# Retention attention and a SwiGLU block on one core: another order for the first 160 steps, and a last block in halves

## The chip, the core and the metric

The kernel runs on one core of a Trainium2 chip. The metric is the device time of one execution in microseconds, so less is better. The engines are TensorE (PE, with its weight loads shown apart as PEld), VectorE (DVE), ScalarE (ACT), GpSimd (POOL) and SyncE (SP), which here only issues transfers. Each engine works through its own queue in order and waits on semaphores where it needs another engine's or a transfer's result.

## What is computed

```python
# q, k, v: (4, 8, 768, 64) float32; gamma per head
for t in range(S):
    state = gamma * state + outer(k[:, :, t], v[:, :, t])
    y[:, :, t] = scale * q[:, :, t] @ state
x = y.transpose(0, 2, 1, 3).reshape(4 * 768, 512)
g, val = x @ w_gate, x @ w_val          # w_gate, w_val: (512, 1536)
out = (silu(g) * val) @ w_out           # w_out: (1536, 512)
```

The three weight matrices come as 64-bit floats, and the kernel converts them itself.

## The kernel before

The 3072 tokens are worked on in four segments (0 to 3) of six blocks of 128 tokens: three chunks of 128 positions of two sequences. Each segment has its attention, an "up" stage (x times the gate and value weights, for 12 pieces of 128 columns of d_ff) and a "down" stage (times w_out). Every float32 product with the weights is made as three matmuls, of operands that are split beforehand into three parts `a` = 0, 1, 2: part 0 by ScalarE (`near_a`, `far_a`), part 1 by VectorE (`near_b`, `far_b`), part 2 by GpSimd or VectorE (`near_c`, `far_c`). In segments 1 to 3 the up stage uses seven block products for eight, from weights that segment 0 has prepared and written to DRAM (`wup`, `wdn`, `wdnt`).

The order of all work is written out by hand in one list, `PLAN`. Its entries are called one after another, and each entry issues its instructions to the queues of its engines, so the list fixes the order within every queue. The start, which is segment 0, has these entries (n is a chunk or a piece of weights):

- On SP, transfers: `l n:w` loads chunk n (w = 0 k transposed, 1 q transposed, 2 v, 3 k; 256 KB each), `A0 A1 A2` the table of decays (256 KB each; A0 and A1 are the mask, A2 the factors for q and k), `U n` and `V n` the 64-bit words of a weight piece (512 KB for each of its halves), `Z n` writes a prepared piece to DRAM, `L` two tiny loads of decay factors.
- Attention of chunk n: `s` scores (TensorE, then two mask products on VectorE), `m` scores times v (TensorE, then ScalarE's part 0 of x), `x n:1` and `x n:2` the other two parts of x (VectorE), `k` or `K` scaling of k on GpSimd or VectorE, `q` or `Q` the same of q, `t` the new state (TensorE, then ScalarE or VectorE), `o` the old state's share (TensorE), `g` decay of the state (ScalarE), `h` copies of the table (ScalarE).
- Weights of piece n: `a`, `b`, `S`, `c`, `C` convert 64-bit words to float32 (a, b, c on ScalarE, S and C on VectorE; for pieces 12 and up, which are w_out, C is on GpSimd), `T` differences of blocks for the seven products (VectorE), `n n:0` to `n n:2` the three parts of the gate weights, `n n:3` to `n n:5` those of the value weights (ScalarE, VectorE, GpSimd in turn).
- Products: `p f:j` gate and `v f:j` value, for pieces 0 and 1 and token blocks j, 12 matmuls each; `u`, `y` their silu and product; `G`, `W`, `i`, `j` the same for the later pieces.

In the down stage `s/D f.tok` (`down`) adds piece f to the bank of token block tok with three matmuls, `s/W f` (`w_load`) loads the split w_out rows of piece f (768 KB), `s/h f` (`h_split`) splits the hidden values, and `s/e tok` (`finish`) scales the finished bank on ScalarE or VectorE and stores it. The last entries of the list are `3/D10.2 3/D11.2 3/e2`: token block 2 is the last. Block 5 of the last segment is already scaled by two engines, a half each, and stored by two transfers.

Of the kernel before, what the change touches and what calls it, by code (L numbers as in the profile page):

```python
# [26 lines left out]
TH = L * P
NSEG = B * NCK // (2 * L)
# [19 lines left out]


PLAN = """  # L50
    l1:0 A2 l0:0 A1 A0 l0:2 U0:0 l2:1 l0:3 s0 a0:1 l2:0 s1 m0 K0 b0:1 V0:0 S0:1 c0:1 l1:2 x0:2 s2
    l1:3 l3:0 x0:1 C0:1 l3:1 k1 U1:1 l2:3 t0 l2:2 l4:0 a0:0 g2 n0:0 Q2 l4:1 n0:1 m1 b0:0 S0:0 c0:0
    n0:2 t1 x1:1 a1:1 l3:3 x1:2 o2 C0:0 a1:0 s3 b1:1 S1:1 l3:2 q3 l5:1 n0:3 n0:4 c1:1 p0:0 l5:2 k2
    l5:0 o3 C1:1 m2 n0:5 t2 s4 b1:0 k3 v0:0 x2:2 S1:0 u0:0 g3 l4:2 U2:0 c1:0 m3 n1:0 U12:3 x2:1 t3
    C1:0 s5 q5 n1:1 h0 q4 o5 o4 x3:1 x3:2 m4 T0:0 n1:3 y0:0 T0:1 m5 p0:1 v0:1 a2 x4:1 u0:1 x5:2 U3:1
    n1:4 T1:0 y0:1 n1:2 T1:1 b2 p1:0 T0:2 U4:0 n1:5 u1:0 a12 Z0 p1:1 a3 x4:2 v1:0 x5:1 v1:1 y1:0
    p0:2 u1:1 v0:2 S2 U5:1 b12 c2 p1:2 u0:2 S12 T1:2 y1:1 C2 n2:0 n2:3 v1:2 y0:2 Z1 b3 n2:1 u1:2
    n2:2 S3 n2:4 T2:0 c3 a4 U13:2 G2:1 C3 y1:2 U6:0 T2:1 n3:0 G2:0 b4 n2:5 n3:1 i2:0 i2:1 T2:2 c12
    W2:0 j2:0 n3:2 W2:1 G3:1 n3:3 S4 C12 a5 Z2 j2:1 Z12 n3:4 c4 C4 U7:1 n3:5 T3:0 T3:1 c13 T3:2 G3:0
    n4:0 n4:1 b5 S5 n4:2 W3:0 n4:3 W3:1 i3:0 i3:1 n4:4 a13 a6 G4:1 c5 Z3 b13 G4:0 T4:0 U8:0 C5 T4:1  # L60
    j3:1 n4:5 b6 U14:3 W4:1 n5:0 T4:2 n5:1 i4:1 n5:2 n5:3 j3:0 S6 i4:0 a7 c6 n5:4 W4:0 T5:0 C6 G5:1
    Z4 T5:1 n6:0 L U9:1 j4:0 n5:5 S13 G5:0 a8 b7 n6:3 T5:2 j4:1 n6:1 c14 C13 W5:1 S7 i5:1 Z5 n6:4
    i5:0 n6:2 j5:1 c7 W5:0 G6:1 n6:5 l4:3 a9 U10:0 C7 n7:0 G6:0 j5:0 i6:1 T6:0 k4 b8 g4 Z13 n7:1
    n7:3 U15:2 S8 n7:2 W6:1 i6:0 c8 n7:4 T7:0 a14 W6:0 C8 l5:3 T7:1 T6:1 b14 G7:1 U11:1 n8:0 n8:1
    n7:5 i7:1 T6:2 G7:0 j6:0 b9 S14 W7:0 h2 c15 j6:1 Z6 S9 C14 n8:3 c9 n8:2 i7:0 n8:4 W7:1 G8:1 T7:2
    C9 G8:0 j7:0 n8:5 a10 b10 n9:0 j7:1 n9:3 Z14 a15 W8:0 P2 W8:1 Z7 n9:4 k5 b15 i8:0 S10 T8:0 n9:1
    i8:1 U16:3 n9:5 c10 S15 P0 T8:1 n9:2 C10 a11 C15 G9:0 t4 G9:1 P1 T9:0 i9:0 T8:2 Z15 j8:1 g5 j8:0
    t5 W9:1 W9:0 b11 n10:0 U17:2 T9:1 c16 Z8 n10:3 1/was0.0 a16 i9:1 n10:1 n10:4 n10:2 b16 G10:1 S11
    n10:5 c11 S16 i10:1 G10:0 0/h0.0 j9:0 C16 Z16 C11 n11:0 W10:0 n11:3 a17 j9:1 i10:0 0/h0.1 b17
# [237 lines left out]
T0, UP0 = 30.0, 8.35  # L307
# [61 lines left out]
def tile_retnet_swiglu(  # L369
# [13 lines left out]
    nc = tc.nc  # L383
# [20 lines left out]
    def f32(t):  # L404
        return t.bitcast(F32)
# [28 lines left out]
    banks = [two[:, ts(i - 4, 512)] if i in (4, 5) else  # L434
             psum.tile([P, 512], F32, name=f"bank{i}") for i in range(8)]
# [532 lines left out]
    def far_a(o, x):  # L968
        act(o[0], x, AF.Copy, scale=CUT)
# [112 lines left out]
    hs, wo = {}, {}  # L1082
# [14 lines left out]
    def w_load(s, t, f, first):  # L1097
        def load():
            wo[f] = item("o", DM)
            o = wo[f].bitcast(U32)  # L1100
            if first:
                nc.sync.dma_start(out=o[:, 2], in_=w_dn[f].bitcast(U32))
            else:
                nc.sync.dma_start(out=o, in_=w_dn3[f])
# [12 lines left out]
    def down(f, tok):
        i, u = divmod(tok, L)
        for a in range(3):
            nc.tensor.matmul(banks[tok], hs[f][:, a, ds(i * TH + u * P, P)], wo[f][:, a],  # L1120
                             start=f == a == 0, stop=f == NF - 1 and a == 2,
                             skip_group_check=True)

    def finish(s, tok):
        i, u = divmod(tok, L)
        p, pos = divmod(s * L, NCK)
        row = (2 * p + i) * S + (pos + u) * P
        t = chunk_x[:, ts(tok % 4, DM)]
        if s == NSEG - 1 and tok > 3:
            t = tmp[:, ts(tok - 4, DM)]  # L1130
        scale = ONE * ONE
        if s == NSEG - 1 and tok == 5:
            a, b = (ds(n * DM // 2, DM // 2) for n in range(2))
            act(t[:, a], banks[tok][:, a], AF.Copy, scale=scale)
            nc.scalar.dma_start(out=out[ds(row, P), a], in_=t[:, a])
            nc.vector.tensor_scalar(t[:, b], banks[tok][:, b], scale, None, op0=mul)
            nc.sync.dma_start(out=out[ds(row, P), b], in_=t[:, b])
            return
        if tok % 2:
            nc.vector.tensor_scalar(t, banks[tok], scale, None, op0=mul)  # L1140
        else:
            act(t, banks[tok], AF.Copy, scale=scale)  # L1142
        nc.sync.dma_start(out=out[ds(row, P)], in_=t)
# [11 lines left out]
    def down_stage(s, t):  # L1155
        nxt = s + 1 if s + 1 < NSEG else None
        table = {**WHEN, **FIRST} if s == 0 else WHEN
        slot_at, steps = [], []
        for n in range(6 * NF):
            f, b = divmod(n, 6)  # L1160
            slot_at.append(t)
            if b == 0:
                steps.append(t)
            if nxt and n in PARTS:
                what, p = PARTS[n]
                d = t + COST[what] + 0.1
                if what == "s":
                    at(t, f"{nxt}/sc{p}", scores_of, p, (R0, R0 + 1) if p else (4, 5))
                    for i in range(2):
                        at(d + 0.1 * i, f"{nxt}/dec{p}.{i}", decayed, p, i)  # L1170
                        at(d + 0.2 + 0.1 * i, f"{nxt}/q{p}.{i}", scale_q2, p, i)
                    if has_old(nxt, p, 0):
                        at(d + 0.6, f"{nxt}/was{p}.0", decay2, nxt, p, 0)
                    if p == 0:
                        at(d + 0.7, f"{nxt}/begin", begin_x, nxt)
                else:
                    k = "ABC".index(what)
                    z = k // 2
                    for i in range(0 if k else 2):
                        at(t - 0.02 + 0.01 * i, f"{nxt}/k{p}.{i}", scale_k2, p, i)  # L1180
                    at(t, f"{nxt}/{what}{p}", (mix_a, mix_b, mix_c)[k], nxt, p)
                    if k != 1 and has_new(nxt, p, z):
                        at(d, f"{nxt}/new{p}.{z}", keep_state, nxt, p, z)
                    if k == 1 and has_new(nxt, p, 1):
                        at(d + 0.9, f"{nxt}/was{p}.1", decay2, nxt, p, 1)
                    for j in range(8 if k else 0):
                        at(d + 0.1 * j, f"{nxt}/y{p}.{z}{j}", bring_y, z, j % 2, j // 2 % 2, j // 4)
                    if k == 2:
                        make_x(d + 1.0, nxt, p, table)
                t += COST[what]  # L1190
            tok = b
            at(t, f"{s}/D{f}.{tok}", down, f, tok)
            t += 3 * PASS_D
            if f == NF - 1:
                at(t + WHEN["end" if nxt else "last"][tok], f"{s}/e{tok}", finish, s, tok)
        for f in range(NF):
            h_split(s, steps[f], f, table["h", f if nxt else NF])
            w_load(s, steps[f], f, s == 0)
        if nxt:
            for n, h in LOADS.items():  # L1200
                at(slot_at[h] + 1.0, f"{nxt}/l{n}", load_pair, nxt, n)
            for f in range(3):
                at(slot_at[UNITS[f]], f"{nxt}/L{f}", load_unit, f)
        return t
# [30 lines left out]
    t = down_stage(0, end)  # L1235
    for s in range(1, NSEG):
# [8 lines left out]
        t = down_stage(s, t)  # L1245
# [50 lines left out]
```

## Time and profile before

| | |
|---|---|
| median of 3 runs | 645.15 us (644.22 to 645.72) |
| the profiled execution | 643.87 us |
| its span, first to last instruction | 642.1 us |
| TensorE busy | 632.8 us, 99% of the span |
| VectorE, ScalarE, GpSimd busy | 76%, 61%, 41% |
| transfers | 140.13 MB, mean 218 GB/s |
| granted TensorE clock | 1.000 |

In the profile's rows a time is in microseconds from the start of the span. In the timeline and the chain a row gives the start, the length, the engine, the line of the kernel and the tile that is written and read; "[1.52 <-DMA x]" says that the engine stood idle for 1.52 us before and that a transfer of x ended this. "SPq" is a transfer's issue on SP's queue; the list of issues gives the size and the time from issue to landing.

### The profile page before, as it was taken

What the parts mean: (1) busy time and instruction counts of PE and PEld (TensorE: products, weight loads), DVE (VectorE), ACT (ScalarE), POOL (GpSimd) and SP (SyncE); (2) the same over time, 40 slices, a digit from 0 to 9 for tenths busy, and PEclk for the clock granted to TensorE, in tenths of its full rate; (3) what the DMA queues carried; (4) which work ended last, traced back from release to release, by engine and by line L of the source; (5) the groups of instructions that cost most, each with busy time, mean ns of one, the idle gap of its engine ahead of it and who ended that gap; (6) DMA issues with size and microseconds to landing.
All of it is one profiled execution on the core that took longest, in us unless ns stands there. A gap on an engine that the chain in (4) does not pass through costs nothing.

```text
span 642.1 us, 14098 instructions
## 1 busy us (share of the span) xinstructions
PE 632.8 (99%) x5576; PEld 580.2 (90%) x5576; DVE 487.8 (76%) x712; ACT 391.8 (61%) x860; POOL 264.5 (41%) x174
## 2 busy tenths in 40 slices
PE   7999999999999999999999999999999999999997
PEld 6899999987779999997778999998777999999886
DVE  4988887999898887665787869675789866778361
ACT  3678797777865565666766555564785555654121
POOL 0625555554436875630003665550101666653000
PEclk9999999999999999999999999999999999999999
DMA  9989988789787445258775640457767444304554
GB/s 320 375 290 338 317 320 290 281 290 328 259 283 298 170 151 173 69 171 270 248 240 213 198 164 8 183 196 247 241 223 264 155 163 173 115 0 157 195 184 170
DMA packets 50050, 140.13 MB, mean 218 GB/s; under 512 B 4928, under 2 KB 17472, under 8 KB 49984
## 3 DMA queue, kind: packets, MB, share of 16 engines
q1 hardware_dynamic: 49552, 138.57, 62.7%
q8 instruction: 44, 0.72, 0.5%
q10 hardware_dynamic: 432, 0.66, 0.3%
q14 instruction: 22, 0.18, 0.1%
HBM read 109.32 MB, written 29.88 MB: 217 GB/s over the span
## 4 chain that ended last, share of the span: by engine, by line
PE 97%; DMA 2%; SPq 0%; POOL 0%; ACT 0%; issue 0%; POOLq 0%
PE bank L1057 41%; PE bank L1120 32%; PE bank L888 13%; PE bank L758 6%; PE bank L906 3%; DMA hT<-in_k_n_dram 1%; DMA tab<-in_decays_dram 1%; PE bank L713 1%; PE bank L699 1%; PE bank L628 1%; PE bank L684 0%; POOL hT L649 0%; SPq L586 0%; SPq L464 0%; ACT chunk_x L1142 0%
## 5 line engine op out<-in xcount | busy, mean ns | idle before, releaser
L1120 PE MATMUL bank<-oitem,gitem 128*128 128x512 f32 x864 | 208.5, 395 | 0.0
L1120 PEld LDWEIGHTS bank<-oitem,gitem 128*128 128x128 f32 x864 | 159.0, 188 | 35.3 <-DMA oitem<-wdnt 0.5
L966 POOL TENSOR_TENSOR gitem<-gitem 128x768 fp32r<-128x768 f32 x72 | 140.6, 1963 | 116.6 <-DVE gitem L963 98.6
L1057 PE MATMUL bank<-xa,gitem 128*128 128x384 f32 x864 | 160.5, 334 | 0.0
L1057 PEld LDWEIGHTS bank<-xa,gitem 128*128 128x128 f32 x864 | 150.8, 188 | 0.2
L966 POOL TENSOR_TENSOR oitem<-oitem 128x256 fp32r<-128x256 f32 (+1 forms) x60 | 65.7, 1102 | 53.0 <-DVE oitem L963 51.2
L1057 PE MATMUL bank<-xb,gitem 128*128 128x384 f32 x432 | 84.5, 334 | 0.0
L888 PE MATMUL bank<-xa,oitem 128*128 128x384 f32 x480 | 84.4, 335 | 0.0
L888 PEld LDWEIGHTS bank<-xa,oitem 128*128 128x128 f32 x480 | 83.0, 188 | 0.4 <-DVE hT L442 0.2
L963 DVE SCALAR_TENSOR_TENSOR gitem<-gitem,loads 128x768 fp32r<-128x768 f32 x72 | 75.1, 1058 | 9.2 <-ACT gitem L960 7.8
L1057 PEld LDWEIGHTS bank<-xb,gitem 128*128 128x128 f32 x432 | 75.9, 188 | 0.4
L960 ACT ACTIVATE gitem<-loads 128x768 fp32r<-128x768 f32 x72 | 59.6, 843 | 25.9 <-PE bank L1057 16.8
L963 DVE SCALAR_TENSOR_TENSOR gitem<-gitem,hT 128x768 fp32r<-128x768 f32 x48 | 46.2, 965 | 25.4 <-ACT gitem L960 25.4
L960 ACT ACTIVATE gitem<-hT 128x768 fp32r<-128x768 f32 x48 | 40.2, 841 | 32.4 <-PE bank L1120 30.2
L991 ACT COPY chunk_x<-bank 64x128 f32<-64x128 f32 x144 | 36.6, 260 | 31.9 <-PE bank L758 21.1
L399 DVE SCALAR_TENSOR_TENSOR gitem<-gitem 128x768 fp32r<-128x768 f32 x48 | 49.1, 1030 | 0.8
L785 POOL TENSOR_TENSOR loads<-loads,tab 128x512 f32<-128x512 f32 x9 | 13.3, 1475 | 81.7 <-PE bank L758 44.6
L1057 PE MATMUL bank<-xb,oitem 128*128 128x384 f32 x216 | 43.4, 335 | 0.0
L1057 PEld LDWEIGHTS bank<-xb,oitem 128*128 128x128 f32 x216 | 38.0, 188 | 0.3
L1074 DVE TENSOR_TENSOR hT<-bank,tmp 128x384 f32<-128x384 f32 x36 | 20.0, 554 | 20.1 <-PE bank L1057 19.9
L963 DVE SCALAR_TENSOR_TENSOR oitem<-oitem,loads 128x256 fp32r<-128x256 f32 (+1 forms) x42 | 34.1, 816 | 0.9 <-ACT oitem L960 0.8
L1072 ACT COPY tmp<-bank 128x384 f32<-128x384 f32 x36 | 17.2, 478 | 27.9 <-PE bank L1057 18.9
(112 smaller groups left out, 792.3 us busy)
## 6 DMA issues: line engine op xcount, KB each, us to landing
loads<-wup SPq DMA_DIRECT2D x36, 896.0 KB, 4.7
oitem<-wdnt SPq DMA_DIRECT2D x36, 768.0 KB, 4.4
wdnt<-oitem SPq DMA_DIRECT2D x12, 768.0 KB, 5.9
wup<-first SPq DMA_DIRECT2D x9, 896.0 KB, 5.5
rawp<-in_w_gate_dram SPq DMA_DIRECT2D x12, 512.0 KB, 6.6
rawp<-in_w_val_dram SPq DMA_DIRECT2D x12, 512.0 KB, 6.2
rawp<-in_w_out_dram SPq DMA_DIRECT2D x12, 512.0 KB, 6.8
out_dram<-chunk_x SPq DMA_DIRECT2D x22, 256.0 KB, 2.2
```

Of the source, the lines that this page charges most:

```text
L399: stt(o, x, 1.0, y, op0=mul, op1=op)
L758: nc.tensor.matmul(o, a, b, start=start, stop=True, skip_group_check=True)
L888: nc.tensor.matmul(o, w[:, a, ts(b, P)], X0[:, a, i, NC - 1 - b], start=a == b == 0, stop=a == 2 and b == NC - 1, skip_group_check=True)
L906: nc.tensor.matmul(o, w[:, a, ts(b, P)], X0[:, a, :, NC - 1 - b, ts(j, P)], start=a == b == 0, stop=a == 2 and b == NC - 1, skip_group_che ...
L960: act(o[0], x, AF.Copy, scale=CUT / FAR)
L963: stt(o[1], f32(o[0]), -FAR, x, op0=mul, op1=add)
L966: op(o[2], f32(o[0]), f32(o[1]), op=add)
L991: copy(cx[half[i], ds(2 * h, 2), c, half[z]], y.rearrange("p (b t) -> p b t", b=2))
L1057: nc.tensor.matmul(o, w[:, a, k], x[:, a, KH - 1 - k], start=start and a == k == 0, stop=a == 2 and k == KH - 1, skip_group_check=True)
L1072: steps = (lambda: copy(p1, x), lambda: tt(c11, z, p1, op=add), lambda: act(gate, c11, AF.Silu, scale=ONE), lambda: copy(u2, x), lambda: c ...
L1074: lambda: copy(p5, wb), lambda: tt(h1, x, p5, op=add),
L1120: nc.tensor.matmul(banks[tok], hs[f][:, a, ds(i * TH + u * P, P)], wo[f][:, a], start=f == a == 0, stop=f == NF - 1 and a == 2, skip_group ...
```

## The change

Three things are changed. The first 160 entries of `PLAN` are put in the order of the kernel that this one was made from; the entries after them keep their order (`L` and `l5:3`, which stood further back, come into the first 160). The last token block of the last segment (`FINAL`, block 2) gets its last three products as six matmuls of half the columns, and its scaling and store as two halves, one on VectorE and SP, one on ScalarE and its queue. Of the w_out loads of the last segment the first three go as two transfers, of two thirds and of one third. `down` gets the segment as an argument for this.

```diff
@@ -48,22 +48,22 @@
 
 
 PLAN = """
-    l1:0 A2 l0:0 A1 A0 l0:2 U0:0 l2:1 l0:3 s0 a0:1 l2:0 s1 m0 K0 b0:1 V0:0 S0:1 c0:1 l1:2 x0:2 s2
-    l1:3 l3:0 x0:1 C0:1 l3:1 k1 U1:1 l2:3 t0 l2:2 l4:0 a0:0 g2 n0:0 Q2 l4:1 n0:1 m1 b0:0 S0:0 c0:0
-    n0:2 t1 x1:1 a1:1 l3:3 x1:2 o2 C0:0 a1:0 s3 b1:1 S1:1 l3:2 q3 l5:1 n0:3 n0:4 c1:1 p0:0 l5:2 k2
-    l5:0 o3 C1:1 m2 n0:5 t2 s4 b1:0 k3 v0:0 x2:2 S1:0 u0:0 g3 l4:2 U2:0 c1:0 m3 n1:0 U12:3 x2:1 t3
-    C1:0 s5 q5 n1:1 h0 q4 o5 o4 x3:1 x3:2 m4 T0:0 n1:3 y0:0 T0:1 m5 p0:1 v0:1 a2 x4:1 u0:1 x5:2 U3:1
-    n1:4 T1:0 y0:1 n1:2 T1:1 b2 p1:0 T0:2 U4:0 n1:5 u1:0 a12 Z0 p1:1 a3 x4:2 v1:0 x5:1 v1:1 y1:0
-    p0:2 u1:1 v0:2 S2 U5:1 b12 c2 p1:2 u0:2 S12 T1:2 y1:1 C2 n2:0 n2:3 v1:2 y0:2 Z1 b3 n2:1 u1:2
-    n2:2 S3 n2:4 T2:0 c3 a4 U13:2 G2:1 C3 y1:2 U6:0 T2:1 n3:0 G2:0 b4 n2:5 n3:1 i2:0 i2:1 T2:2 c12
-    W2:0 j2:0 n3:2 W2:1 G3:1 n3:3 S4 C12 a5 Z2 j2:1 Z12 n3:4 c4 C4 U7:1 n3:5 T3:0 T3:1 c13 T3:2 G3:0
-    n4:0 n4:1 b5 S5 n4:2 W3:0 n4:3 W3:1 i3:0 i3:1 n4:4 a13 a6 G4:1 c5 Z3 b13 G4:0 T4:0 U8:0 C5 T4:1
-    j3:1 n4:5 b6 U14:3 W4:1 n5:0 T4:2 n5:1 i4:1 n5:2 n5:3 j3:0 S6 i4:0 a7 c6 n5:4 W4:0 T5:0 C6 G5:1
-    Z4 T5:1 n6:0 L U9:1 j4:0 n5:5 S13 G5:0 a8 b7 n6:3 T5:2 j4:1 n6:1 c14 C13 W5:1 S7 i5:1 Z5 n6:4
+    l0:0 l1:0 A0 A1 s0 U0:0 l0:2 l0:3 a0:1 s1 b0:1 A2 h0 S0:1 m0 K0 x0:2 c0:1 l2:0 x0:1 l2:1 l1:3
+    C0:1 t0 l1:2 V0:0 l3:1 n0:0 s2 a0:0 Q2 l3:0 l2:3 n0:1 b0:0 S0:0 m1 k1 x1:1 x1:2 l2:2 c0:0 n0:2
+    U1:1 C0:0 t1 o2 l3:3 g2 s3 n0:3 n0:4 l4:1 p0:0 m2 a1:1 x2:1 k2 q3 b1:1 l4:0 a1:0 x2:2 S1:1 l5:1
+    l3:2 n0:5 c1:1 k3 t2 C1:1 o3 b1:0 l5:0 l4:2 g3 v0:0 s4 S1:0 t3 l5:2 c1:0 C1:0 U2:0 m3 s5 U12:3
+    U3:1 q5 q4 u0:0 a2 o5 o4 T0:0 n1:0 m4 b2 y0:0 x3:1 x3:2 m5 T0:1 n1:1 n1:3 T0:2 S2 n1:2 p0:1 v0:1
+    n1:4 T1:0 x4:1 u0:1 y0:1 a12 n1:5 x5:1 U4:0 T1:1 a3 p1:0 x4:2 u1:0 p1:1 x5:2 Z0 u1:1 T1:2 c12
+    v1:0 U5:1 y1:0 v1:1 p0:2 Z1 l5:3 v0:2 c2 C2 b12 y1:1 p1:2 n2:0 a4 U6:0 u0:2 b3 n2:1 u1:2 v1:2
+    S12 n2:3 L y0:2 S3 c3 n2:2 U13:2 G2:0 n2:4 T2:0 G2:1 C3 y1:2 T2:1 n3:0 b4 n2:5 n3:1 i2:0 i2:1
+    T2:2 W2:0 j2:0 n3:2 W2:1 G3:1 n3:3 S4 C12 a5 Z2 j2:1 Z12 n3:4 c4 C4 U7:1 n3:5 T3:0 T3:1 c13 T3:2
+    G3:0 n4:0 n4:1 b5 S5 n4:2 W3:0 n4:3 W3:1 i3:0 i3:1 n4:4 a13 a6 G4:1 c5 Z3 b13 G4:0 T4:0 U8:0 C5
+    T4:1 j3:1 n4:5 b6 U14:3 W4:1 n5:0 T4:2 n5:1 i4:1 n5:2 n5:3 j3:0 S6 i4:0 a7 c6 n5:4 W4:0 T5:0 C6
+    G5:1 Z4 T5:1 n6:0 U9:1 j4:0 n5:5 S13 G5:0 a8 b7 n6:3 T5:2 j4:1 n6:1 c14 C13 W5:1 S7 i5:1 Z5 n6:4
     i5:0 n6:2 j5:1 c7 W5:0 G6:1 n6:5 l4:3 a9 U10:0 C7 n7:0 G6:0 j5:0 i6:1 T6:0 k4 b8 g4 Z13 n7:1
-    n7:3 U15:2 S8 n7:2 W6:1 i6:0 c8 n7:4 T7:0 a14 W6:0 C8 l5:3 T7:1 T6:1 b14 G7:1 U11:1 n8:0 n8:1
-    n7:5 i7:1 T6:2 G7:0 j6:0 b9 S14 W7:0 h2 c15 j6:1 Z6 S9 C14 n8:3 c9 n8:2 i7:0 n8:4 W7:1 G8:1 T7:2
-    C9 G8:0 j7:0 n8:5 a10 b10 n9:0 j7:1 n9:3 Z14 a15 W8:0 P2 W8:1 Z7 n9:4 k5 b15 i8:0 S10 T8:0 n9:1
+    n7:3 U15:2 S8 n7:2 W6:1 i6:0 c8 n7:4 T7:0 a14 W6:0 C8 T7:1 T6:1 b14 G7:1 U11:1 n8:0 n8:1 n7:5
+    i7:1 T6:2 G7:0 j6:0 b9 S14 W7:0 h2 c15 j6:1 Z6 S9 C14 n8:3 c9 n8:2 i7:0 n8:4 W7:1 G8:1 T7:2 C9
+    G8:0 j7:0 n8:5 a10 b10 n9:0 j7:1 n9:3 Z14 a15 W8:0 P2 W8:1 Z7 n9:4 k5 b15 i8:0 S10 T8:0 n9:1
     i8:1 U16:3 n9:5 c10 S15 P0 T8:1 n9:2 C10 a11 C15 G9:0 t4 G9:1 P1 T9:0 i9:0 T8:2 Z15 j8:1 g5 j8:0
     t5 W9:1 W9:0 b11 n10:0 U17:2 T9:1 c16 Z8 n10:3 1/was0.0 a16 i9:1 n10:1 n10:4 n10:2 b16 G10:1 S11
     n10:5 c11 S16 i10:1 G10:0 0/h0.0 j9:0 C16 Z16 C11 n11:0 W10:0 n11:3 a17 j9:1 i10:0 0/h0.1 b17
@@ -1101,7 +1101,8 @@
             if first:
                 nc.sync.dma_start(out=o[:, 2], in_=w_dn[f].bitcast(U32))
             else:
-                nc.sync.dma_start(out=o, in_=w_dn3[f])
+                for i in (slice(2), slice(2, 3)) if s == NSEG - 1 and f < 3 else (slice(None),):
+                    nc.sync.dma_start(out=o[:, i], in_=w_dn3[f][:, i])
 
         def o():
             return [wo[f][:, i] for i in range(3)]
@@ -1114,12 +1115,17 @@
             at(t + c, f"{s}/d{f}.2", lambda: far_c(o(), f32(o()[2])))
             at(t + z, f"{s}/Z{f}", lambda: nc.sync.dma_start(out=w_dn3[f], in_=wo[f].bitcast(U32)))
 
-    def down(f, tok):
+    halves_of = [ds(n * DM // 2, DM // 2) for n in range(2)]
+    FINAL = 2
+
+    def down(s, f, tok):
         i, u = divmod(tok, L)
-        for a in range(3):
-            nc.tensor.matmul(banks[tok], hs[f][:, a, ds(i * TH + u * P, P)], wo[f][:, a],
-                             start=f == a == 0, stop=f == NF - 1 and a == 2,
-                             skip_group_check=True)
+        final = s == NSEG - 1 and f == NF - 1 and tok == FINAL
+        for cols in halves_of if final else [slice(None)]:
+            for a in range(3):
+                nc.tensor.matmul(banks[tok][:, cols], hs[f][:, a, ds(i * TH + u * P, P)],
+                                 wo[f][:, a, cols], start=f == a == 0,
+                                 stop=f == NF - 1 and a == 2, skip_group_check=True)
 
     def finish(s, tok):
         i, u = divmod(tok, L)
@@ -1130,11 +1136,18 @@
             t = tmp[:, ts(tok - 4, DM)]
         scale = ONE * ONE
         if s == NSEG - 1 and tok == 5:
-            a, b = (ds(n * DM // 2, DM // 2) for n in range(2))
+            a, b = halves_of
             act(t[:, a], banks[tok][:, a], AF.Copy, scale=scale)
             nc.scalar.dma_start(out=out[ds(row, P), a], in_=t[:, a])
             nc.vector.tensor_scalar(t[:, b], banks[tok][:, b], scale, None, op0=mul)
             nc.sync.dma_start(out=out[ds(row, P), b], in_=t[:, b])
+            return
+        if s == NSEG - 1 and tok == FINAL:
+            a, b = halves_of
+            nc.vector.tensor_scalar(t[:, a], banks[tok][:, a], scale, None, op0=mul)
+            nc.sync.dma_start(out=out[ds(row, P), a], in_=t[:, a])
+            act(t[:, b], banks[tok][:, b], AF.Copy, scale=scale)
+            nc.scalar.dma_start(out=out[ds(row, P), b], in_=t[:, b])
             return
         if tok % 2:
             nc.vector.tensor_scalar(t, banks[tok], scale, None, op0=mul)
@@ -1189,7 +1202,7 @@
                         make_x(d + 1.0, nxt, p, table)
                 t += COST[what]
             tok = b
-            at(t, f"{s}/D{f}.{tok}", down, f, tok)
+            at(t, f"{s}/D{f}.{tok}", down, s, f, tok)
             t += 3 * PASS_D
             if f == NF - 1:
                 at(t + WHEN["end" if nxt else "last"][tok], f"{s}/e{tok}", finish, s, tok)
```

## The prediction

> **What bounds the kernel now.** I read the page first, then the chain of work that ended last, then the first 35 us and the last 10 us of the timeline.
>
> ```profile
> span 642.1 us, 14098 instructions
> PE 632.8 (99%) x5576; PEld 580.2 (90%) x5576; DVE 487.8 (76%) x712; ACT 391.8 (61%) x860; POOL 264.5 (41%) x174
> PE 97%; DMA 2%; SPq 0%; POOL 0%; ACT 0%; issue 0%; POOLq 0%
> ```
>
> TensorE (PE) is busy all but 9.3 us of the span (642.1 less 632.8). A change that leaves the amount of matmul alone can only work on those 9.3 us, or add to them. The chain in order of time says where they lie:
>
> ```profile
> 8.06 7.49 DMA hT<-in_k_n_dram
> ...
> 15.69 1.05 POOL hT L649
> ...
> 16.79 0.69 PE bank L684 x16
> 17.48 1.02 PE bank L699 x16
> 18.50 1.09 PE bank L628 x16
> 19.59 1.62 PE bank L906 x12
> ...
> 22.23 1.02 PE bank L713 x16
> 23.25 0.47 PE bank L684 x16
> ...
> 29.01 1.89 PE bank L699 x32
> 30.90 1.90 PE bank L713 x32
> 32.80 14.59 PE bank L906 x120
> ...
> 590.66 47.66 PE bank L1120 x210
> 638.34 0.60 ACT chunk_x L1142
> ```
>
> From 16.79 until ScalarE's copy at 638.34 the chain is TensorE alone, one step after another without a hole that counts. Ahead of it stands one load (a k_n chunk, issued at 8.06, landed at 15.55), then GpSimd's scaling of it (step k1), then the matmuls that use it (t1). So two places count: what makes TensorE unbroken at the start, and what follows its last matmul.
>
> In these rows s (scores) is L628, t (state) L684, o (old state) L699, m (mix) L713, p and v (first gate and value products) L906. Their costs on the chain are 1.09, 0.47 (0.69 once), 1.02, 1.02 and 1.62 us.
>
> The start is bound by loading:
>
> ```profile
> 5.00:10.00 5.00, 3.33 (x30) 3.36 (x32) 1.22 (x2) 0.00 (x0) 0.00 (x0) 1.00 1.05 382
> 20.00:25.00 5.00, 5.00 (x77) 4.51 (x76) 4.33 (x9) 3.90 (x7) 2.83 (x4) 1.00 1.05 386
> 12.04 0.69 DVE L649 TENSOR_TENSOR hT<-hT,tab 128x512 f32<-128x512 f32 x1 [0.43 <-DMA hT<-in_k_n_dram]
> 12.84 1.16 PE L628 MATMUL bank<-hT 64*128 64x128 f32 x16 [1.52 <-DMA hT<-in_k_t_dram]
> 14.92 1.09 PE L713 MATMUL bank<-tmp,hT 128*64 128x128 f32 x16 [0.30 <-DMA hT<-in_v_n_dram]
> 22.16 0.85 PEld L713 LDWEIGHTS bank<-tmp,hT 128*64 128x64 f32 x16 [0.17 <-DMA hT<-in_v_n_dram]
> ```
>
> The last two columns of the windows are the DMA share (full) and GB/s. At 386 GB/s a block of 256 KB (a chunk, or a third of the table) takes 262,144 B / 386 GB/s = 0.68 us and a weight half twice that. One queue, SP's, issues nearly all of it, so a load lands when its place in the queue comes up. Counting places in 256 KB in the old order: l2:0 is place 11, l1:2 place 14, l1:3 place 15 and l2:2 place 23; the rows show them at about 12.8, 14.9, 15.55 and 22.1. The bytes do not change, so the same places should land at the same times in the new order, whoever stands in them.
>
> **The change, part by part: the first 160 steps.** TensorE's own order changes little: t0 goes ahead of s2, m2 and t2 ahead of o3, v0:0 ahead of s4. What changes is the places:
> - l1:2 goes from 14 to 13, l1:3 from 15 to 12, l2:2 from 23 to 19, V0 from 13 to 15; a block of the table, A2, from 2 to 9.
> - l3:0 is at 17 (was 16), l4:0 at 26 (was 24), l3:2 at 28 (was 27), l5:0 at 29 (was 30).
>
> t0, now ahead of s2, waits for K0 on VectorE (0.69), and K0 for the late A2: place 9, 15.55 - 6 x 0.68 = 11.5, so K0 ends at 12.2 and t0 at about 12.8, which is when s2 can start anyway. t1, the step that released everything before, now has k_n at 12: 15.55 - 3 x 0.68 = 13.5, plus 1.05 of GpSimd = 14.6. m1 has its v at 14.2 and runs to 15.3, so t1 runs right behind it, 15.3 to 15.9, and not at 16.79. o2 needs Q2 on VectorE, behind the two mask products of s2:
>
> ```profile
> 14.93 0.70 ACT L532 ACTIVATE first<-rawp 128x512 f32<-128x512 f32 x1
> 16.44 0.84 DVE L643 TENSOR_TENSOR loads<-hT,tab 128x512 f32<-128x512 f32 x1
> 17.57 0.59 ACT L535 ACTIVATE bank<-first 128x512 int32<-128x512 f32 x1
> 18.20 0.70 DVE L545 SCALAR_TENSOR_TENSOR bank<-first,bank 128x512 uint32<-128x512 uint32 x1 [0.28 <-ACT bank L535]
> 18.93 0.69 ACT L538 ACTIVATE first<-rawp 128x512 int32<-128x512 uint32 x1 [0.76 <-DVE bank L545]
> 20.00 0.68 DVE L553 CUSTOM_DVE_ANT_0 first<-bank,first 128x1024 uint16<-128x1024 uint16 x1
> 20.60 1.27 DVE L634 TENSOR_TENSOR tmp<-bank,tab 128x512 f32<-128x512 f32 x2
> 22.27 0.61 ACT L960 ACTIVATE oitem<-first 128x512 fp32r<-128x512 f32 x1
> 23.74 1.27 POOL L966 TENSOR_TENSOR oitem<-oitem 128x512 fp32r<-128x512 f32 x1 [1.36 <-DVE oitem L963]
> ```
>
> s2 keeps its data at places 10 and 11 and so its 12.84; its products end at 14.0, the masks 1.27 later, Q2 0.84 later: 16.1. o2 runs 16.1 to 17.1. What is late next is l3:0: place 17, 15.55 + 2 x 0.68 = 16.9. So s3 starts at 17.1 (18.50 before). Behind it: s3 1.09, p0:0 1.62, m2 1.02, t2 0.47, o3 1.02, v0:0 1.62, to 23.9. l4:0 at place 26 lands at 22.1 + 3 x 0.68 = 24.1: s4 to 25.2, t3 to 25.7. l3:2 at place 28 is there at 25.5, m3 ends at 26.7; s5 has l5:0 at 26.2 and ends at 27.8; o5 and o4 1.89 and m4 and m5 1.90 more: 31.6. Then p0:1 starts, the first of the 120 matmuls that began at 32.80. **Gain 1.2 us, and I take 1.1**, since several steps (s4, s5) come to rest within 0.3 us of what releases them.
>
> The conversions must keep up. For the value weights (V0, place 15, 15.55) the steps above are a, b, S, c, C, n:3 and n:5, in this order by time except that a is the first row; n:4 is another 0.68 on VectorE. In the new order: a to 16.25, b 16.85, S 17.55, c 18.25; C waits behind two splits of x (0.68 each) to 19.5; n0:3 20.1; behind the mask products of s3, n0:4 at 21.4; n0:5 at 22.7. v0:0 starts at 22.3 and needs that last part after two thirds, at 23.4. That is 0.7 us of cover; when it is gone TensorE waits.
>
> After 31.6 everything is to arrive 1.1 us earlier than before. The tightest place I found in the old order is G2:1:
>
> ```profile
> 46.39 1.30 POOL L966 TENSOR_TENSOR oitem<-oitem 128x512 fp32r<-128x512 f32 x1 [9.20 <-DVE oitem L963]
> 47.11 12.97 PEld L888 LDWEIGHTS bank<-xa,oitem 128*128 128x128 f32 x75
> ```
>
> GpSimd ends at 47.69, and the product wants that part eight matmuls after 47.1, about 48.5: 0.8 us spare, less than the gain. But the new order puts a2, b2 and S2 well ahead of the splits of x (S2 was step 132, now 106), so the conversion for G2 ends earlier too. On ScalarE a2 now waits for U2, place 35, 22.1 + 12 x 0.68 = 30.3, with n1:0, m4's copy, b2 and m5's copy queued behind it; a2 is twice the 0.70 row, so n1:0 starts at about 31.7, and p1:0, which wants it, comes at 31.6 + 2 x 1.46 = 34.5: hidden. The moves of L (two tiny loads), l5:3 (256 KB, no wait in front of it), h0 (a copy on ScalarE ahead of m0's copy, while that waits for its matmuls) and c12 I cost at nothing: ScalarE is busy 61% of the span. Without that cover c12 would cost two of the 0.69 row, 1.4 us, and l5:3 one place, 0.7.
>
> **The last block in halves.** Rows of the old end, where another block (tok 5) is in halves already:
>
> ```profile
> 636.11 0.38 ACT L1134 ACTIVATE tmp<-bank 128x256 f32<-128x256 f32 x1
> 636.52 0.42 DVE L1136 TENSOR_SCALAR tmp<-bank 128x256 f32<-128x256 f32 x1 [2.93 <-ACT tmp L1134]
> ...
> out_dram<-chunk_x SPq DMA_DIRECT2D x1, 256.0 KB, 2.0
> ...
> out_dram<-tmp ACTq DMA_DIRECT2D x1, 128.0 KB, 2.1
> ```
>
> VectorE had been idle for 2.93 us, and the block's products were done, since ScalarE was at its half already; yet VectorE's half began only when that ended: the two halves of one bank went one behind the other. In the change the order is VectorE first, ScalarE second. So behind the last matmul come 0.42 + 0.03 + 0.38 = 0.83 us in place of 0.60: +0.23. The six half-width matmuls cost 6 x 14.59/120 = 0.73 against 3 x 47.66/210 = 0.68: +0.05. The store is half as long but lands no sooner, 2.1 against 2.0: +0.1. **Tail +0.35.** Bounds: with all halves free of each other, VectorE's would lie beside the second half's matmuls, and only ScalarE's 0.38 stays: +0.05 - 0.22 + 0.1 = -0.07.
>
> The rows show two readers of a bank in series; none shows a reader of one half while TensorE writes the other. Here the Trainium skill (PSUM — Partial Sum Buffer, section "PSUM bank collisions raise a hardware error") speaks against the change: two engines on one bank and quadrant collide even at disjoint columns, TensorE's writes included, so accesses are kept apart in time. By that rule VectorE's half would wait for all six matmuls, and the tail is the +0.35; by halves alone it would be the -0.07. No run yet shows the mixed pair.
>
> **Three w_out loads in two.**
>
> ```profile
> oitem<-wdnt SPq DMA_DIRECT2D x36, 768.0 KB, 4.4
> 590.50 6.78 PE L1120 MATMUL bank<-oitem,gitem 128*128 128x512 f32 x29
> 590.74 0.32 SPq L1104 DMA_DIRECT2D oitem<-wdnt  x1
> ```
>
> W2 is issued at 590.74 and lands at 595.1; its first product is the tenth block of three matmuls after 590.50, at 590.50 + 27 x 0.227 = 596.6. One more issue of 0.32 us fits in 1.5 us. SP has only stores of finished blocks and later loads behind it. Cost 0; without that cover, 0.3 each.
>
> **Sum.** Profiled execution: 643.87 us, of which 642.1 is the span. -1.1 + 0.35 = -0.75, so 643.1 there. The three runs have the median 645.15, 1.28 above the profiled one; against it the forecast is 645.15 - 0.75 = **644.4 us**.
>
> **The rivals.**
> - *The halves overlap* (-0.07, not +0.35): 645.15 - 1.1 - 0.1 = 643.95. For it: the products of the two halves are separate groups. Against: the 2.93 us row. Chance 0.2.
> - *The gain is used up on the way*: some conversion between 35 and 130 us, not TensorE, turns out to set the pace, and only some 0.2 us of the lead are left; with the tail 645.3. For it: 0.8 us spare at G2:1. Against: no wait there now, VectorE and ScalarE both get the weights of G2 earlier. Chance 0.17.
> - *Slower: the value weights come too late.* V0 lands about 1.4 us later than before. From its a (14.93) to the end of n0:5 (23.74 + 1.27) the old rows take 10.1 us, because work for other pieces stood between. If the new order kept those 10.1, n0:5 would end at 25.7, v0:0 could start at 24.6 instead of 22.3, and p0:1, 9.1 us of steps later, at 33.7, 0.9 later than before; with the tail 645.15 + 1.25 = 646.4, and more if k3, next on GpSimd, holds up t3 as well. It decides once n0:5 ends after 23.4. Against: in the old order g2, a1:1, a1:0 and b1:1 stood on ScalarE inside this chain, in the new one they stand behind n0:3 (g2 alone before it). Chance 0.18.
> - *The places mean nothing*: loads land as before whatever their order, and only the tail acts: 645.5. Against: four rows that fit one line. Chance 0.05.
>
> **How the numbers follow.** Forecast 0.4. Its own doubt is about 0.9 us either way: if only l3:0 binds, p0:1 starts at 31.4 and the start gives 1.4; each block that lands later than its place takes 0.7. A measurement of this kernel tells about 0.2%, 1.3 us, from no change: the bounds are 643.86 and 646.44. Faster: half of the overlap case (0.1) and some 0.4 of the forecast's (0.17): 0.27. Slower: half of the late weights (0.1), and as much again from the tails of the used-up lead and the others: 0.2. Same: 0.53. The range goes from 643.1 (overlap, and a start 0.8 better) to 646.4 (the late weights as priced) and leaves out what lies above.
>
> **What would show it.** s3 at about 17.1 and p0:1 at about 31.6; t1 no longer on the chain; a load (l3:0, l4:0 or l3:2) as the last wait. At the end VectorE's half starting after the last matmul, ScalarE's after VectorE's, and about 4 us from last matmul to end of span. Wrong: p0:1 later than 32.8, n0:5 ending after 23.4, a wait of TensorE between 35 and 130 us, or VectorE's half starting under the last three matmuls.

## The result, and the profile after

The changed kernel takes 643.19 us in the median (642.66 to 644.22), the kernel before 645.2 us in the same comparison (644.22 to 645.72). The ratio is 0.9971, 95% interval 0.9959 to 0.9982: faster by 2.0 us, with 1.2 to 2.6 inside the interval. The forecast was 644.4, in a range of 643.1 to 646.4; the time lies at its lower edge, and the sign went to the case that had been given 0.27.

The profiled execution of the changed kernel took 642.91 us, that of the one before 643.87: 0.96 less. The page after, its first lines:

```profile
span 641.1 us, 14110 instructions
PE 631.2 (98%) x5579; PEld 579.5 (90%) x5579; DVE 485.6 (76%) x713; ACT 392.2 (61%) x860; POOL 265.4 (41%) x174
PE 94%; DMA 4%; ACT 0%; DVE 0%; SPq 0%; issue 0%; ACTq 0%
```

TensorE is still the bound; the holes are 9.9 us (641.1 less 631.2), no smaller than before. What changed is where the chain begins to be TensorE alone. The chain in order of time, after, as the profile puts it together:

```profile
6.96 6.04 DMA hT<-in_k_n_dram
...
13.02 9.00 DMA rawp<-in_w_gate_dram
...
22.04 0.69 ACT first L532
...
22.75 0.61 ACT bank L535
...
23.38 0.71 DVE bank L545
...
24.11 0.68 ACT first L538
...
24.81 0.70 DVE first L553
...
25.65 0.69 PE bank L684 x16
26.33 0.88 PE bank L713 x16
27.21 1.09 PE bank L628 x16
28.30 1.89 PE bank L699 x32
30.19 1.90 PE bank L713 x32
32.09 0.91 PE bank L906 x6
```

Before, a k_n chunk and GpSimd's scaling released TensorE at 16.79. Now TensorE is unbroken from t3 on, at 25.65. p0:1, the last row, starts at 32.09 and not at 32.80: 0.71 us won. The timeline has the same stretch with its waits:

```profile
16.61 1.16 PE L628 MATMUL bank<-hT 64*128 64x128 f32 x16
17.70 1.70 PE L906 MATMUL bank<-xa,oitem 128*128 128x256 f32 x12
20.90 1.27 POOL L966 TENSOR_TENSOR oitem<-oitem 128x512 fp32r<-128x512 f32 x1 [1.15 <-DVE oitem L963]
21.84 1.69 PE L906 MATMUL bank<-xa,oitem 128*128 128x256 f32 x12
24.18 1.16 PE L628 MATMUL bank<-hT 64*128 64x128 f32 x16 [0.65 <-DMA hT<-in_k_t_dram]
25.65 0.69 PE L684 MATMUL bank<-hT 128*64 128x64 f32 x16 [0.30 <-DVE first L553]
```

These are s3, p0:0, the last part n0:5 of the first value weights, v0:0, s4 and t3. Up to s4 it went as forecast, to 0.1 us, or a little better; t3 came 0.45 later than forecast.

What releases t3 has to be read with care. The chain names a weight transfer, the gate half of U1, and its five conversion steps (a1:1, b1:1, S1:1, c1:1, C1:1), because C1:1 is what ended last before t3 began. But t3 does not need C1:1. In the kernel C1:1 reads bank 7 and t3 writes bank 6; and in `l4_first`, a version with two loads exchanged (below), TensorE had passed its wait for VectorE ahead of t3 at 25.70, by the trace's record of that wait, while C1:1 ended at 26.53 (in `u1_early` 25.95 and 26.78). What t3 does need is l3:2, the v of chunk 3. It was issued at 17.23 and landed at 25.40, and the first matmul of t3 began 0.25 us later. The same 0.25 stands between that landing and t3 in the two other traces in which t3 waits: 25.27 and 25.52 in `all_again`, 25.45 and 25.70 in `a2_late`. So the last wait of the start is one for a load, l3:2.

The end of the span, after:

```profile
636.32 1.32 PE L1126 MATMUL bank<-oitem,gitem 128*128 128x512 f32 x8
637.68 0.42 DVE L1147 TENSOR_SCALAR chunk_x<-bank 128x256 f32<-128x256 f32 x1 [0.70 <-PE bank L1126]
638.14 0.38 ACT L1149 ACTIVATE chunk_x<-bank 128x256 f32<-128x256 f32 x1 [2.34 <-DVE chunk_x L1147]
638.55 0.35 ACTq L1150 DMA_DIRECT2D out_dram<-chunk_x  x1
...
out_dram<-chunk_x ACTq DMA_DIRECT2D x1, 128.0 KB, 1.7
```

VectorE's half begins when all matmuls are done (637.64), ScalarE's when VectorE's is done; the two are in series. Even so, from the last matmul's end to the end of the span it is 3.48 us; before it was 3.78.

So the two profiled executions differ by 0.71 at the start, 0.30 at the end and 0.15 between 47 and 128 us, less 0.20 between there and the last matmul, where only the one after waits 0.30 us for a w_out load of an earlier segment (at 309.7). That makes the 0.96, but the median fell by 2.0. The experiments look for the rest.

### The profile page after: what moved, and what is told of

It reads as the page before. It is cut to its first block, busy times and chain, and to the rows that moved or that the text cites. A ratio compares the mean times of both kernels' runs of the same rounds, so it can differ in the third digit from the quotient of the medians.

```text
span 641.1 us, 14110 instructions
## 1 busy us (share of the span) xinstructions
PE 631.2 (98%) x5579; PEld 579.5 (90%) x5579; DVE 485.6 (76%) x713; ACT 392.2 (61%) x860; POOL 265.4 (41%) x174
## 4 chain that ended last, share of the span: by engine, by line
PE 94%; DMA 4%; ACT 0%; DVE 0%; SPq 0%; issue 0%; ACTq 0%
PE bank L1057 41%; PE bank L1126 31%; PE bank L888 13%; PE bank L758 6%; PE bank L906 2%; DMA rawp<-in_w_gate_dram 1%; DMA oitem<-wdnt 1%; DMA hT<-in_k_n_dram 1%; DMA hT<-in_q_t_dram 1%; PE bank L713 0%; PE bank L684 0%; PE bank L699 0%; PE bank L628 0%; SPq L464 0%; DVE bank L545 0%
## 5 line engine op out<-in xcount | busy, mean ns | idle before, releaser
L888 PE MATMUL bank<-xa,oitem 128*128 128x384 f32 x480 | 84.2, 335 | 0.0
L888 PEld LDWEIGHTS bank<-xa,oitem 128*128 128x128 f32 x480 | 83.0, 188 | 0.2
```

Source lines behind the costliest of these rows:

```text
L888: nc.tensor.matmul(o, w[:, a, ts(b, P)], X0[:, a, i, NC - 1 - b], start=a == b == 0, stop=a == 2 and b == NC - 1, skip_group_check=True)
```

## The experiments

All ratios are to the kernel before, run on the same chip.

### Each part alone

`order_only` is the kernel before with `PLAN` in the new order (the two lists differ up to their 171st entry), `halves_only` has only the last block in halves, `split_only` only the split loads (the edits are those parts of the diff above), `all_again` is the changed kernel once more.

> Only the first 160 steps in the other order; the end and the w_out loads are those of before. Theory A (the start frees TensorE earlier, as the trace of after shows: p0:1 at 32.1 and not at 32.8): 0.7 us faster than before, ratio 0.9989, and the last matmul near 637.6. Theory B (the order also takes away waits in the middle that the profiled execution of before did not show): 1.5 us or more, ratio 0.9977 or less. Rival C (the median moved because of the end): no change, ratio 0.9997 to 1.0003.

> Only the last block's products, scaling and store in halves; order and loads are those of before. Theory A (the trace of after: 0.3 us less from the last matmul to the end of the span): 0.3 us faster, ratio 0.9995. The prediction's tail: 0.35 us slower, ratio 1.0005. Rival C (the end carries most of the change): 1.2 us faster, ratio 0.998.

> Only the first three w_out loads of the last segment in two transfers each. Theory A: no change, ratio 0.9998 to 1.0002, because TensorE waits for none of these loads in either trace. Rival D (in executions that were not profiled TensorE does wait for them, and a part that lands first helps): 1 us faster, ratio 0.9985.

> The changed kernel once more, beside its parts. All theories: ratio 0.996 to 0.998 as measured before. If the parts add up (theory A) their differences sum to this one's; by theory A alone that sum is 1.0 us, ratio 0.9985, so 1 us would be missing and lies in waits that differ from one execution to the next.

| | median | ratio | 95% |
|---|---|---|---|
| `order_only` | 643.92 | 0.9976 | 0.9959 to 0.9993 |
| `halves_only` | 644.80 | 0.9984 | 0.9967 to 1.0000 |
| `split_only` | 644.87 | 0.9989 | 0.9971 to 1.0007 |
| `all_again` | 643.70 | 0.9972 | 0.9956 to 0.9987 |

The order carries most of it. Its interval still holds the 0.9989 that the start alone would give. The three parts sum to 3.3 us and the whole is 1.9; with intervals of about 1 us either way, that is no contradiction and no proof that they add up. The interval of `halves_only` just leaves out the 1.0005 of the prediction's tail. The split loads are not told from nothing, and no trace shows TensorE waiting for a load of the last segment's first three pieces, before or after. The traces of the two kernels with the old order brought what the first profile had hidden, a wait of TensorE in the middle, here in `halves_only`:

```profile
54.43 2.44 POOL L555 TENSOR_TENSOR first<-first,rawp 128x1024 int32<-128x1024 int32 x1 [0.59 <-ACT rawp L538]
58.27 0.56 SPq L511 DMA_DIRECT2D rawp<-in_w_gate_dram  x1
65.82 1.12 ACT L538 ACTIVATE first<-rawp 128x1024 int32<-128x1024 uint32 x1 [1.08 <-DMA rawp<-in_w_gate_dram]
68.45 0.55 DVE L442 TENSOR_TENSOR hT<-bank,tmp 128x384 f32<-128x384 f32 x1
69.05 2.18 PE L888 MATMUL bank<-xa,oitem 128*128 128x384 f32 x11 [0.60 <-DVE hT L442]
```

Read from above: GpSimd's conversion C12 ends at 56.9; behind it, and behind the store Z12, SP issues U7 (58.27); ScalarE's step c5 waits for that transfer's landing (1.08); then C5 and T4:1 and only then j3:1 on VectorE; and j3:1 frees the bank that the product W4:1 wants. In `split_only` the same product waits 0.53 us at 68.65.

### What of the order makes the start shorter

Two theories: A, the places of the loads alone bring the gain (which is how the prediction reckoned it); E, the order of TensorE's steps does. `loads_only` gives the loads their new places and keeps all other steps in the old order; `compute_only` is the reverse. For the first lines of each:

```diff
 # loads_only
-    l1:0 A2 l0:0 A1 A0 l0:2 U0:0 l2:1 l0:3 s0 a0:1 l2:0 s1 m0 K0 b0:1 V0:0 S0:1 c0:1 l1:2 x0:2 s2
+    l0:0 l1:0 A0 A1 U0:0 l0:2 l0:3 A2 l2:0 s0 a0:1 l2:1 s1 m0 K0 b0:1 l1:3 S0:1 c0:1 l1:2 x0:2 s2
 # compute_only
+    l1:0 A2 l0:0 A1 A0 s0 l0:2 U0:0 a0:1 s1 b0:1 l2:1 h0 S0:1 m0 l0:3 K0 x0:2 c0:1 x0:1 l2:0 V0:0
```

> Before, with the first 26 loads in the new order and the compute steps in the old one. Theory A (the places of the loads give the start): TensorE unbroken earlier, p0:1 at 32.1 to 32.3 (32.8 before, 32.1 in after), t1 no longer the releasing step. Rival E (the new order of the compute steps gives it): p0:1 at 32.7 or later. The rest as in the old order: the cover of W4:1 stays thin, a wait of 0.5 us near 68 in some executions.

> Before, with the compute steps in the new order and the first 26 loads in the old one. Theory A: p0:1 at 32.6 to 33.0, no earlier than before, since the k_n chunk of t1 lands at 15.55 again. Rival E: p0:1 at 32.1. Theory F for the middle (a2, b2 and S2 early bring the conversion of all later pieces ahead): no wait of TensorE between 47 and 127, and GpSimd's C12 begins by 52.5 and not at 54.2.

Measured: `loads_only` 646.04 us, 1.0016 (1.0003 to 1.0028); `compute_only` 646.51, 1.0019 (1.0006 to 1.0032). Each half alone is slower than the kernel before; both theories fall. In `loads_only` p0:1 starts at 33.5, in `compute_only` at 34.1. What TensorE waited for, a row of each:

```profile
24.09 1.16 PE L628 MATMUL bank<-hT 64*128 64x128 f32 x16 [0.89 <-DMA hT<-in_k_t_dram]
```

```profile
22.17 1.09 PE L713 MATMUL bank<-tmp,hT 128*64 128x128 f32 x16 [1.49 <-DMA hT<-in_v_n_dram]
```

In the first, s4 stands ahead of v0:0 as in the old order and waits for l4:0 at its new, later place; in the new order v0:0's 1.62 us come first and fill most of that time. (s2 and o2 wait too, 1.65 and 1.22, and the stretches of p0:0 and v0:0 are 0.48 and 0.28 longer than before.) In the second, m2 stands ahead of o3 as in the new order and waits for l2:2 at its old place 23. As I read these waits, the gain is in the pairing: where a load went back, another product was put ahead of its user, and where a step went ahead, its load did.

`loads_only` also has the wait of the middle, 1.02 us near 70. `compute_only` has none between 47 and 127, as expected, but its C12 began at 53.71 and not by 52.5: its whole start is 1.3 us late.

### The middle

Theory F: the wait near 69 us goes because a2, b2 and S2 stand early in the new order; with them the whole row of conversions, C12 and U7 runs some 2.5 us earlier. The rows after, to be held against the five above:

```profile
51.66 2.44 POOL L555 TENSOR_TENSOR first<-first,rawp 128x1024 int32<-128x1024 int32 x1
55.48 0.55 SPq L511 DMA_DIRECT2D rawp<-in_w_gate_dram  x1
62.32 1.15 ACT L538 ACTIVATE first<-rawp 128x1024 int32<-128x1024 uint32 x1
64.97 0.55 DVE L442 TENSOR_TENSOR hT<-bank,tmp 128x384 f32<-128x384 f32 x1
```

j3:1 ends at 65.52. W4:1 is due 21.0 us after the first L888 matmul (69.05 less the wait of 0.60, less 47.48 in `halves_only`), so at 67.5 here: 2.0 us to spare. In the profile of before j3:1 ended at 67.69 and W4:1 was due at 68.2: 0.5 to spare, and U7's landing varies by more than that: issued at 57.95 to 58.27, it landed at 63.77 before, at 65.31 in `split_only` and at 65.71 in `halves_only`. `a2_late` is `order_only` with a2, b2 and S2 back beside their old neighbours (one line of it; b2 and S2 stand in the next two):

```diff
-    U3:1 q5 q4 u0:0 a2 o5 o4 T0:0 n1:0 m4 b2 y0:0 x3:1 x3:2 m5 T0:1 n1:1 n1:3 T0:2 S2 n1:2 p0:1 v0:1
+    U3:1 q5 q4 u0:0 o5 o4 T0:0 n1:0 m4 y0:0 x3:1 x3:2 m5 T0:1 n1:1 n1:3 T0:2 n1:2 p0:1 v0:1 a2 n1:4
```

> The new order alone, with three conversion steps of piece 2 (a2, b2, S2) back beside the steps they stood beside in the old order. Theory F: the start stays, p0:1 at 32.1, but the middle is as in the old order again: the two halves of U7 are issued near 57 and not at 55, c5 waits for them, and TensorE stands 0.3 to 0.8 us near 68 in the profile. Rival G (the thin place is due to c12 alone, or to chance): U7 at 55.0 to 55.5 and no wait.

Its trace:

```profile
57.09 0.55 SPq L511 DMA_DIRECT2D rawp<-in_w_gate_dram  x1
64.61 1.12 ACT L538 ACTIVATE first<-rawp 128x1024 int32<-128x1024 uint32 x1 [2.11 <-DMA rawp<-in_w_gate_dram]
67.84 2.35 PE L888 MATMUL bank<-xa,oitem 128*128 128x384 f32 x12 [0.31 <-DVE hT L442]
```

U7 is issued 1.6 us later than after, and the wait is back. The mechanism of the wait is shown. The time, 643.85 us and 0.998 (0.9969 to 0.9992), is not told from `order_only`.

`j3_first` attacks the same wait from the other side, in the kernel before:

```diff
-    ... T4:0 U8:0 C5 T4:1 j3:1 n4:5 ...
+    ... T4:0 U8:0 j3:1 C5 T4:1 n4:5 ...
```

> The old order with one entry moved: j3:1 stands ahead of C5 on VectorE instead of behind C5 and T4:1. Theory F (in the old order the wait of TensorE near 68 to 70 us comes from U7's late transfer by way of c5, C5, T4:1 and j3:1): the wait at W4:1 is gone, the stage from the first L888 to the first L758 takes about 80.8 us (81.7 in three traces of the old order), p0:1 stays at about 32.8, and the ratio to before is about 0.9985. Rival: U7's late landing holds TensorE at another place (T4's or n5's consumers, G5, W5), the stage stays at 81.7 and the ratio is 1.000.

The wait near 69 us is gone from its trace, but there is another, which the profile puts down to ScalarE and which was not followed further:

```profile
80.88 3.41 PE L888 MATMUL bank<-xa,oitem 128*128 128x384 f32 x18 [0.20 <-ACT tmp L442]
```

The stage from the first L888 to the first L758 took 81.37 us, between the 80.8 of the theory and the 81.7 of the rival, and the time was 645.21 us, 1.0005 (0.9987 to 1.0023): the 0.9985 that theory F expected lies just outside. So the place is right, its price for the median is not shown. Over all traces that stage takes 80.78 to 80.83 in the eight whose steps stand in the new order with an early a2, 81.50 in `a2_late`, and 80.94, 81.37, 81.69, 81.79 and 82.2 in the five with the old order. The profile of before was the luckiest of the five. Leaving out `j3_first` (81.37) and `loads_only` (82.2), whose steps or loads were moved, the middle is worth 0.15 to 1.0 us; with 0.71 and 0.30 that makes 1.2 to 2.0 of the 2.0 measured (1.2 to 2.6). Which part of the spread the middle takes in the median stays open.

One rival for the missing part can be put aside: spells of half clock (last section) that hit one order more than the other. Among runs with the same mean clock, taken together over the two chips of the experiments, the new order is ahead all the same. With 0.999 or 1.000 the medians are 645.08 us for the 44 runs of before and 643.89 for the 16 of `order_only`, `all_again`, `a2_late` and `act_store`; with 0.996 or 0.997 they are 645.09 (32 runs) and 643.68 (19).

### The end

The tail came out at -0.30 where +0.35 had been forecast. Theory H: it is the queue, since the last store now goes by ScalarE's. The rival: it is the size of the store. `act_store` is `order_only` with the last, whole store on ScalarE's queue:

```diff
-        nc.sync.dma_start(out=out[ds(row, P)], in_=t)
+        (nc.scalar if s == NSEG - 1 and tok == 2 else nc.sync).dma_start(out=out[ds(row, P)], in_=t)
```

> The new order, the last block whole again (512 columns, ScalarE), but its store issued from ScalarE's queue and not SP's. Theory H (what made the tail shorter in after is the queue of the last store: it lands in 1.73 us and not 2.03, and the program's closing waits then end on it): from the last matmul to the end of the span 3.3 us (3.8 before, 3.4 after), ratio to before 0.997 or less. Rival J (the halves made it shorter): 3.8 us as before.

Its trace, and that of `halves_only`, which has the halves at the end of the old order, in the list of issues of the last microseconds:

```profile
out_dram<-chunk_x ACTq DMA_DIRECT2D x1, 256.0 KB, 2.1
```

```profile
out_dram<-chunk_x SPq DMA_DIRECT2D x1, 128.0 KB, 1.8
out_dram<-chunk_x ACTq DMA_DIRECT2D x1, 128.0 KB, 1.7
```

Theory H falls: 256 KB take 2.0 to 2.1 us on either queue, 128 KB take 1.7 to 1.8 on either. The tail from the last matmul's end was 3.8 us in `act_store` and `order_only`, 3.47 in `all_again` and 3.68 in `halves_only`. The time of `act_store`, 644.27 us and 0.9982 (0.9968 to 0.9997), says no more.

The size of the store is not the whole answer either. In `split_only` the last block is whole, and yet its tail is 3.56. Up to the last landing the tails are nearly alike: 2.69 us before, 2.64 after, 2.65 in `halves_only`, 2.67 in `split_only`. What differs is the rest, 1.10, 0.84, 1.02 and 0.90 us. SP ends the program with five waits for transfers, one behind the other, 0.06 us each if there is nothing to wait for; 5, 1, 4 and 2 of them, in the same order, come behind the last landing in these traces. So the halves gain 0.05 us by themselves, and 0.26 of the 0.30 is how many of these waits happened to be left over.

### Two loads moved by hand

The chain after names U1, the wait of s4 names l4:0. Three versions were made on the chain's word: if these two bind, the start can be made shorter still. `l4_first` exchanges l4:0 and l3:3, `u1_early` puts U1:1 ahead of l2:2, `u1_l4` does both:

```diff
-    ... x1:1 x1:2 l2:2 c0:0 n0:2 U1:1 C0:0 t1 o2 l3:3 g2 ... q3 b1:1 l4:0 a1:0 ...
+    ... x1:1 x1:2 U1:1 l2:2 c0:0 n0:2 C0:0 t1 o2 l4:0 g2 ... q3 b1:1 l3:3 a1:0 ...
```

> The changed kernel with l4:0 and l3:3 in each other's places (l4:0 two places of 0.68 us earlier). If the place of l4:0 binds the start, as the prediction had it, s4 starts at about 23.5 instead of 24.18 and p0:1 at about 31.5. If the conversion of the second gate half binds (U1's transfer, a1:1, b1:1, S1:1, c1:1, C1:1, then the bank for t3), s4 starts earlier, t3 stays at about 25.6 and p0:1 at 32.0 to 32.1. The span says nothing at this size.

> The changed kernel with U1:1 issued ahead of l2:2, one place of 0.68 us earlier (l2:2 two places later, about 19.7). If the conversion of the second gate half binds t3: C1:1 ends at about 24.8 instead of 25.51, t3 starts right behind s4 at about 25.3 instead of 25.65, and p0:1 at about 31.75. m2 waits for l2:2 some 0.4 us, which the wait of s4 takes up. If it does not bind: t3 at 25.6 and p0:1 at 32.1, or later by the 0.4.

> Both of these, timed. If s4's load and U1's conversion are the two chains that bind here: s4 at about 23.9 (behind m2's 0.4), t3 at 25.0 to 25.2 (k3's scaling of the l3:3 that now lands at about 24.1 ends at about 25.2), p0:1 at about 31.6, a span 0.4 us shorter than that of the changed kernel, ratio to before 0.9965. If not: p0:1 at 32.1 and 0.997. The interval will hardly tell these ratios apart; the trace's start does.

`u1_l4` took 644.78 us, 0.9995 (0.9979 to 1.0011): what the change had won is mostly gone. The reason stands in its chain:

```profile
12.91 9.14 DMA hT<-in_v_n_dram
...
22.10 1.09 PE L713 MATMUL bank<-tmp,hT 128*64 128x128 f32 x16 [2.28 <-DMA hT<-in_v_n_dram]
```

The expectation was wrong in its count: U1:1 issues both of its halves, four places and not two, so l2:2 went from place 19 to 23. It landed at 22.06, which is where place 23 had been in the old order (22.1). m2 waited for it, 2.28 us instead of 0.4; after that wait the granted clock was 0.82 to 0.84 from 20 to 30 us, and p0:1 started at 35.4.

`l4_first` (644.58 us, once) and `u1_early` (645.07, once) did not decide between s4's load and U1's conversion. In both TensorE waited for nothing from t0 until p0:1, and yet p0:1 started at 33.2 and 33.4, because TensorE itself ran slower. One row of the windows of `l4_first` and the same one of after; the third column from the right is the granted clock:

```profile
10.00:15.00 5.00, 4.03 (x49) 3.44 (x46) 3.38 (x6) 2.76 (x6) 1.04 (x1) 0.62 1.07 377
```

```profile
10.00:15.00 5.00, 3.92 (x76) 3.42 (x74) 4.54 (x8) 2.94 (x6) 1.04 (x1) 1.00 1.06 375
```

In the same busy time 49 matmuls went through and not 76. But their records of TensorE's waits settle that C1:1 does not hold t3 (see the result). l3:2, which does, kept its place 28 in all three versions. So none of them could show what an earlier t3 would bring, and a version with l3:2 at an earlier place was not run. None of these versions came out faster than the changed kernel.

## Why the prediction was right or wrong

- *What bounds the kernel.* Right: only the start and the end could move, and TensorE without a hole in between. But "no wait there now" was read from one execution, in the middle from one that was better than the others. That execution (643.87 us) was below all seven timed runs of before in the comparison (644.22 to 645.72); the text had named this difference of 1.28 us and asked no further.
- *The start, -1.1; measured -0.71.* The rule of places held: s3 at 16.61 (forecast 17.1), v0:0 at 21.84 (22.3), s4 at 24.18 (24.1), n0:5 done at 22.17 (22.7), l3:2 landed at 25.40 (25.5). The forecast that a load (l3:0, l4:0 or l3:2) would be the last wait came true with l3:2. The step that failed is "s4 to 25.2, t3 to 25.7": t3 was given no releaser but s4. The text says "l3:2 at place 28 is there at 25.5", but charges it to m3 alone; t3, ahead of m3, multiplies by the same v. The sum could have been made from the rows of before; t3 started at 25.65, not 25.2, and the 0.4 goes on to p0:1.
- *The tail, +0.35; measured -0.30.* The order in series was right, and the 0.42 and 0.38 are there. VectorE's half waited until all six matmuls were done, though its columns were done after three, as it would by the PSUM rule of the Trainium skill that was cited (PSUM — Partial Sum Buffer, section "PSUM bank collisions raise a hardware error"). The trace shows how: only the last of the six matmuls raises the semaphore that VectorE waits for, and ScalarE waits for VectorE's. So the program keeps the accesses apart; what the chip would do if they overlapped, no run here shows. Two terms failed. "It lands no sooner, 2.1" was taken from stores of block 5, which had 256 KB stores beside them; with the other half beside it 128 KB landed in 1.73 us, 0.3 less than the 256 KB (2.03). And the end of the span behind the landing was held to be fixed: it fell from 1.10 to 0.84 us, as only one of SP's closing waits was left and not five. That second term is luck: in `halves_only` four were left (1.02).
- *Three loads in two, 0.* Right as far as 0.9989 (0.9971 to 1.0007) can say.
- *The rivals.* "The halves overlap" did not happen, though its tail is the nearer one. "The gain is used up on the way" turned round: the conversions that it feared were a cost of the old order, and the new one has 2.0 us to spare there and not 0.5. "The value weights come too late" did not happen; n0:5 ended 0.5 us ahead of its forecast. "The places mean nothing" is refuted by `loads_only` and `u1_l4`, which lose by places alone.
- *The chances.* The forecast's 644.4 is 1.2 us too high: about 0.65 from the tail, 0.15 to 1.0 from the middle, less 0.4 from the start. Two errors of opposite sign and one thing unseen came out inside the range; that is luck in part.

## What to carry to other kernels

Before a chain is costed, list for each step all that it reads, and charge a load to the first step that reads it; the one that nobody charged is the one that binds next. A profile names what ended last before a step as its releaser; whether the step needs it is told by the program, or by a trace in which it ended later. When the orders of loads and of their users were made for each other, half of one with half of the other is worse than either, so such a change is tested whole and in parts. And a stage with half a microsecond to spare in one profile has to be looked at in several before it is called free of waits.

## What the runs showed that was not expected

- A half clock early in the span. In `l4_first` the granted clock was 0.62 from 10 to 15 us and 0.70 in the next 5; in `order_only` 0.72 and 0.94, in after 1.00 throughout. In all of them m0 waited about 2.5 us for its v_n just before. 0.28 and 0.06 of 5 us at half the pace are 3.4 us in `order_only`, one spell of a fixed length (3.41 by the trace's record of the clock; 6.83 in `l4_first`), and there it cost nothing, as TensorE was waiting for loads anyway (p0:1 at 32.05). Two such spells in `l4_first` cost 1.1 us. Of 46 timed runs of four kernels with the new order 11 had a mean clock of 0.994 or 0.995; their medians were 645.0 and 644.5 us, against 643.5 to 644.0 for those with 0.996 to 1.000. The Trainium skill (TensorE: Matmul & The Clock Gate, section on the HAM clock gate) has the clock halved after an idle window of some 3.4 us that runs free of the kernel. The length agrees; here a wait of 2.45 us, shorter than the window, sometimes had that result.
- A last store took 1.7 to 1.8 us for a half of 128 KB, with the other half beside it, and 2.0 to 2.1 for 256 KB, on either queue.
